# w2's row pairs one by one, its first piece in two halves of the partitions, c and x in three transfers each

## The chip, the cores, the metric

One core of one Trainium2 chip. Times are device microseconds (us) of whole executions. The profile is one execution taken by the hardware profiler; its span runs from the first to the last instruction and is about 2 us shorter than the time.

## The reference

A decoding step for one token: a condition `c` gives six modulation vectors; a layer norm, attention over a cache of 32,768 positions (32 query heads, 8 key and value heads of 128), a projection; then a second layer norm and a feed-forward layer of 1792 units. Only the sizes matter here: 149.4 MB are read once, and there is little arithmetic for each byte.

```python
mod = (silu(c) @ w_mod).reshape(1, 6, 1, -1)     # sa, ca, ga, sb, cb, gb
h = layernorm(x) * (1 + ca) + sa
x = x + ga * attention(h, k_cache, v_cache, wq, wo)
h = layernorm(x) * (1 + cb) + sb
x = x + gb * (maximum(h @ w1, 0) @ w2)           # w1 (512, 1792), w2 (1792, 512)
```

## The kernel before

Every load goes through one queue, in one fixed order, issued by SyncE: w_mod, c, x, wq, the K and V cache, wo, w1, w2. wo, w1 and w2 come in pieces of falling size, so that the arithmetic behind the last byte is short.

```python
FB = 2; FA = FT // FB                                    # 14 row blocks of w2 = 7 row pairs
W2P = [(0, 2, slice(0, FB)), (2, FA - 5, slice(0, FB)), (FA - 3, 1, slice(0, FB)), (FA - 2, 1, slice(0, FB)),
       (FA - 1, 1, slice(0, 1)), (FA - 1, 1, slice(1, FB))]
W1P = [(0, KT - 1), (KT - 1, KT)]
# ... in load():
    a0, n, bs = W2P[key[1]]
    # t: [128, n, nb, 512] in the slot of w1 and w2
    src = w2_v[:, a0:a0 + n, bs]
stream_dma(t[:], src)                                    # all kinds of loads
# ...
stream_dma(cx_row[0:8], c[0].rearrange("(a n) -> a n", a=8))
stream_dma(cx_row[8:16], A_x[0, 0].rearrange("(a n) -> a n", a=8))
```

The end of the program: w1's product, ReLU into `hid_bd`, then w2's product in 56 matmuls, which wait for w2 piece by piece. `keep_clock(n)` issues n matmuls whose result nobody reads; what it is meant for is in its name (in the run keep_clock, five more went with a clock of 1.00 in place of 0.50 behind them).

```python
for part, (k0, k1) in enumerate(W1P):
    w1_f = need(("w1", part))...
    for kt in range(k0, k1):
        for ft in range(FT):
            nc.tensor.matmul(hidT_ps[:, ft:ft + 1], lhsT=w1_f[...], rhs=h2T[:, kt:kt + 1], ...)
        if kt < KT - 2:
            keep_clock(1)
nc.scalar.activation(out=hid_bd ..., in_=hidT_ps ..., func=ACT.Relu)
keep_clock(1)
for part, (base, n, bs) in enumerate(W2P):
    w2_sb = need(("w2", part))
    # 8 matmuls for a row pair: out ffn_ps [4, 128]
# o_rows = ffn_ps * gb_rows; o_bf = o_rows + x1_rows
nc.sync.dma_start(out=out[0, 0]..., in_=o_bf[:])
```

Of the kernel before, what the change touches and what calls it, by code (L numbers as in the profile page):

```python
# [17 lines left out]
def kernel(  # L18
# [15 lines left out]
    P = 128  # L34
# [16 lines left out]
    FB = 2  # L51
    FA = FT // FB

    W2P = [(0, 2, slice(0, FB)), (2, FA - 5, slice(0, FB)), (FA - 3, 1, slice(0, FB)), (FA - 2, 1, slice(0, FB)),
           (FA - 1, 1, slice(0, 1)), (FA - 1, 1, slice(1, FB))]
    W1P = [(0, KT - 1), (KT - 1, KT)]
    assert Dh == 128 and REP == 4 and D == 512 and Dff % (FB * P) == 0 and NTILE == 4
    scale = float(Dh) ** -0.5
# [9 lines left out]
    def wo_v(i):  # L68
        g0, n = WOP[i]
        return A_wo[g0 * REP * Dh:(g0 + n) * REP * Dh, :].rearrange("(p r) d -> p r d", p=P)  # L70
# [24 lines left out]
    def piece(name, at, n):  # L95

        if name not in pieces:
            pieces[name] = ring.tile([P, 2 * TK * Dh], BF16, tag="slot", name=name)
        return pieces[name][:, at:at + n]

    def load(key):
        kind = key[0]
        if kind == "wm":
            t = ring.tile([P, KT, 6 * D], BF16, tag="slot", name="wm_sb")
            src = wm_v
        elif kind == "wq":
            t = ring.tile([P, KT, Hq * Dh], BF16, tag="slot", name="wq_sb")
            src = wq_v
        elif kind in "kv":
            g, steps = key[1], key[2]  # L110
            src = (kv if kind == "k" else vv)[g, :, TK * steps[0]:TK * (steps[-1] + 1), :]
            name = "Ksb" if kind == "k" else "Vsb"
            if len(steps) == 2:
                t = ring.tile([P, TK * len(steps), Dh], BF16, tag="slot", name=name)
            else:
                t = piece(name, TK * Dh * (steps[0] % 2), TK * Dh).rearrange("p (j d) -> p j d", d=Dh)
        elif kind == "wo":
            g0, n = WOP[key[1]]
            t = piece("wo_sb", g0 * REP * D, n * REP * D).rearrange("p (r d) -> p r d", d=D)
            src = wo_v(key[1])  # L120
        elif kind == "w1":
            k0, k1 = W1P[key[1]]
            t = piece("w12_sb", k0 * Dff, (k1 - k0) * Dff).rearrange("p (kt f) -> p kt f", f=Dff)
            src = w1_v[:, k0:k1]
        else:
            a0, n, bs = W2P[key[1]]
            nb = bs.stop - bs.start
            t = piece("w12_sb", KT * Dff + (a0 * FB + bs.start) * D, n * nb * D)
            t = t.rearrange("p (a b d) -> p a b d", a=n, b=nb)
            src = w2_v[:, a0:a0 + n, bs]  # L130
        stream_dma(t[:], src)
        if kind in "kv":
            for i, u in enumerate(steps):
                loaded[(kind, g, u)] = t[:, TK * i:TK * (i + 1), :]
        else:
            loaded[key] = t[:]

    def stream_dma(dst, src):
        i = nc.sync.dma_start(out=dst, in_=src)  # L139
        tc.stamp_issue_order_token(i.ins, "sp_stream")  # L140
        if last_loop:

            tc.add_manual_dep(i.ins, last_loop[0], mybir.DependencyInfo(
                mybir.DependencyClass.NoSync, mybir.DependencyReason.DATA))
# [5 lines left out]
    stream += [("v", LAST, (0, 1)), ("v", LAST, (2,)), ("v", LAST, (3,))] + [("wo", i) for i in range(len(WOP))]  # L150
    stream += [("w1", i) for i in range(len(W1P))] + [("w2", i) for i in range(len(W2P))]
    pos = [0]

    def need(key):
        while key not in loaded:
            load(stream[pos[0]])
            pos[0] += 1
        return loaded[key]
# [1 line left out]

    wm_sb = need(("wm",))
    cx_row = const.tile([16, D // 8], BF16)
    stream_dma(cx_row[0:8], c[0].rearrange("(a n) -> a n", a=8))
    stream_dma(cx_row[8:16], A_x[0, 0].rearrange("(a n) -> a n", a=8))

    ident_bf = const.tile([P, P], BF16)
    make_identity(nc, ident_bf[:])
# [8 lines left out]
    for hp in range(4):  # L176
        h, par = hp // 2, hp % 2
        src = AP(ib.tensor, ib.offset + 64 * h + par, [[ib.ap[0][0], P], [0, 4], [2, 32]])
# [67 lines left out]
    def bank(name):  # L246
        return ps_s.tile([P, 512], F32, tag="s", name=name)[:]
# [360 lines left out]
    with tc.manual_schedule(engines={mybir.EngineType.PE, mybir.EngineType.DVE}):  # L608
# [125 lines left out]
        ffn_ps = bank("ffn_ps")[0:KT, 0:P]  # L734
        last = len(W2P) - 1
        for part, (base, n, bs) in enumerate(W2P):
            w2_sb = need(("w2", part))
# [43 lines left out]
```

## Time and profile before

| | |
|---|---|
| time, median of 6 runs (lowest to highest) | 355.96 us (355.69 to 356.53) |
| span | 353.7 us |
| share of the DMA engines' time that packets took | 98.4% |

(The prediction was made from the first three runs, with a median of 355.84.) The DMA engines are busy to the end; the prediction shows the lines. This table, by stretches of the tail: start and end of the stretch, its length, busy us (and instructions) of each engine, granted TensorE clock, busy share of the DMA engines, GB/s.

```profile
core 0: us, PE busy (x) PEld busy (x) DVE busy (x) ACT busy (x) POOL busy (x), PEclk, DMA share, GB/s
344.00:346.00 2.00, 2.00 (x42) 1.23 (x41) 0.57 (x3) 0.12 (x1) 0.00 (x0) 1.00 1.03 400
346.00:348.00 2.00, 1.53 (x42) 1.49 (x40) 0.00 (x0) 0.29 (x1) 0.00 (x0) 1.00 1.04 396
348.00:350.00 2.00, 1.84 (x34) 1.71 (x32) 0.00 (x0) 0.00 (x0) 0.00 (x0) 1.00 0.57 209
350.00:352.00 2.00, 0.71 (x13) 0.53 (x10) 0.56 (x2) 0.00 (x0) 0.00 (x0) 1.00 0.00 0
```

The DMA moves 400 and 396 GB/s up to 348 us and has moved its last byte before 350.

### The profile page before, as it was taken

The numbers are of one execution on the slowest core, as the hardware profiler recorded it, in microseconds if no ns is written. First come the engines' busy times: TensorE is split into PE (matmuls) and PEld (weight loads), VectorE is DVE, ScalarE is ACT, GpSimd is POOL, SyncE is SP. The second block draws the span as 40 slices with busy tenths as digits, with TensorE's granted clock in tenths as the row PEclk, the third lists the DMA queues.
The fourth block names the chain that finished last, engine by engine and source line by source line (L and its number), as shares of the span: only waits on it lengthen the run. The fifth ranks groups of instructions, "written<-read, shape, count | busy, mean of one in ns | idle before, by whom it ended". The sixth has DMA issues, their size and how long they took to land. (4 is left out here: it accounts for less than half of the span.)

```text
span 353.7 us, 4064 instructions
## 1 busy us (share of the span) xinstructions
PE 278.1 (79%) x1348; PEld 111.8 (32%) x1351; DVE 207.3 (59%) x269; ACT 28.2 (8%) x68; POOL 8.5 (2%) x14
## 2 busy tenths in 40 slices
PE   0352781999898979897969797979789787989995
PEld 0121230333343423332323233333333233334445
DVE  8555774882868268472949177553938095743050
ACT  1212004000110011001100101010100010020000
POOL 9000000000000000000000000000000000000000
PEclk9995997799899999999999998999999999999999
DMA  8999999999999999999999999999999999999994
GB/s 317 450 419 452 432 412 437 448 419 424 459 419 422 445 437 421 437 441 419 437 448 419 424 459 416 426 436 437 422 434 445 426 424 448 430 422 422 423 418 186
DMA packets 7076, 149.59 MB, mean 423 GB/s; under 512 B 792, under 2 KB 1048, under 8 KB 2200
## 3 DMA queue, kind: packets, MB, share of 16 engines
q1 hardware_dynamic: 7064, 149.43, 98.4%
q8 instruction: 8, 0.13, 0.1%
q14 instruction: 4, 0.03, 0.0%
HBM read 149.42 MB, written 0.00 MB: 422 GB/s over the span
## 5 line engine op out<-in xcount | busy, mean ns | idle before, releaser
L411 DVE STREAM_TRANSPOSE KTt<-Ksb 128x2048 f32<-128x2048 f32 x64 | 143.2, 2283 | 66.5 <-DMA Ksb<-in_A_k_cache_dram 58.8
L493 PE MATMUL o_ps<-Vsb,PT_g 128*16 (+1 forms) x512 | 128.0, 382 | 22.4 <-ACT qbd L395 9.5
L431 PE MATMUL S_ps<-KTt,qbd 128*128 128x512 bf16 x512 | 122.5, 391 | 22.2 <-DVE KTt L411 20.6
L431 PEld LDWEIGHTS <-qbd 128*128 128x128 bf16 x512 | 49.0, 98 | 87.0 <-issue 29.1
L493 PEld LDWEIGHTS o_ps<-Vsb,PT_g 128*16 x416 | 35.9, 86 | 90.7 <-issue 66.4
L437 DVE TENSOR_SCALAR_CACHE_REDUCE S_g<-S_ps 128x512 f32<-128x512 f32 x16 | 11.0, 690 | 27.7 <-PE S_ps L431 27.7
L395 ACT COPY qbd<-qrep_sb 32x128 bf16<-32x128 bf16 x32 | 9.4, 295 | 139.0 <-PE S_ps L431 137.9
L474 DVE STREAM_TRANSPOSE PT_g<-P_g 128x1024 bf16<-128x1024 bf16 x8 | 9.7, 1218 | 6.6 <-ACT P_g L468 6.6
L465 ACT ACTIVATE nbias<-Mb_ps 128x1 f32<-128x1 f32 x8 | 1.4, 171 | 131.1 <-PE Mb_ps L463 131.1
L493 PEld LDWEIGHTS <-PT_g 128*16 128x16 bf16 x96 | 8.2, 90 | 11.0
L233 PE MATMUL xc_ps<-cx_sel,cx_bd 16*128 16x2 bf16 x4 | 0.3, 172 | 12.8 <-DVE cx_bd L227 12.8
L468 ACT ACTIVATE P_g<-S_g,nbias 128x1024 bf16<-128x1024 f32 x8 | 9.2, 1148 | 0.2
L524 DVE SCALAR_TENSOR_TENSOR Y<-o_ps,smask,Y 16x128 f32<-16x128 f32 x24 | 8.1, 339 | 0.8
L179 DVE COPY sel<-ident_bf 128x128 bf16<-128x128 bf16 x4 | 7.6, 3730 | 0.0
L480 PE MATMUL L_ps<-Lexp,ones_f 128*128 128x4 f32 x16 | 3.0, 257 | 4.3 <-DVE Lexp L477 4.3
L606 PE MATMUL spare_ps<-qbd,ident_bf 128*128 128x512 bf16 x16 | 5.1, 380 | 0.2 <-issue 0.2
L449 PE MATMUL mT_ps<-ident_f,m_p 128*1 128x128 f32 x8 | 2.2, 270 | 3.9 <-DVE m_p L446 2.0
L452 DVE TENSOR_REDUCE Mrow<-mT_ps 1x4 f32<-1x128 f32 x8 | 2.1, 257 | 5.3 <-PE mT_ps L449 5.3
L480 PEld LDWEIGHTS L_ps<-Lexp,ones_f 128*128 128x128 f32 x16 | 3.1, 222 | 5.7 <-issue 5.1
L543 DVE TENSOR_TENSOR oT_sb<-acc_ps,Linv 128x4 bf16<-128x4 f32 x8 | 1.2, 151 | 5.7 <-PE acc_ps L530 5.7
L514 DVE MEMSET o_ps<- 16x512 f32 x8 | 3.9, 485 | 0.8
L561 DVE CAST o_sb<-o_ps 128x4 bf16<-128x4 f32 (+2 forms) x4 | 0.7, 166 | 6.1 <-PE o_ps L557 6.1
(112 smaller groups left out, 85.2 us busy)
## 6 DMA issues: line engine op xcount, KB each, us to landing
Ksb<-in_A_k_cache_dram SPq DMA_DIRECT2D x16, 4096.0 KB, 29.2
Vsb<-in_A_v_cache_dram SPq DMA_DIRECT2D x15, 4096.0 KB, 24.5
wq_sb<-in_A_wq_dram SPq DMA_DIRECT2D x1, 4096.0 KB, 18.8
Vsb<-in_A_v_cache_dram SPq DMA_DIRECT2D x2, 2048.0 KB, 23.4
wm_sb<-in_w_mod_dram SPq DMA_DIRECT2D x1, 3072.0 KB, 10.4
wo_sb<-in_A_wo_dram SPq DMA_DIRECT2D x1, 2048.0 KB, 25.1
w_sb<-in_B_w_dram SPq DMA_DIRECT2D x1, 1344.0 KB
wo_sb<-in_A_wo_dram SPq DMA_DIRECT2D x1, 1024.0 KB, 27.0
```

The costliest lines, as they stand in the source:

```text
L179: nc.vector.tensor_copy(out=sel[:, hp, :].rearrange("p (a c) -> p a c", a=4), in_=src)
L395: nc.scalar.copy(out=o, in_=i)
L411: t = nc.vector.transpose(out=KTt[:].bitcast(F32), in_=Ksb[:, 32 * half:32 * half + 32, :].rearrange("p j d -> p (j d)").bitcast(F32),)
L431: nc.tensor.matmul(S_ps_tiles[g], lhsT=qbd[g % 2][:, hp, s, :], rhs=KTv[:, 16 * sl:16 * sl + 16, h, :, par], start=(t4 == 0 and sl == 0 an ...
L437: nc.vector.tensor_scalar(out=S_tiles[g][:, G, :], in0=S_ps_tiles[g], scalar1=1.0, scalar2=None, op0=ALU.mult, op1=ALU.max, accum_out=m_ti ...
L468: nc.scalar.activation(out=P_g[:], in_=S_g[:].rearrange("p g f -> p (g f)"), func=ACT.Exp, bias=nbias[:], scale=scale, accum_out=l_g[:],)
L474: nc.vector.transpose(out=PT_g[:], in_=P_g[:])
L480: nc.tensor.matmul(L_ps[:], lhsT=ones_f[:], rhs=Lexp[:], start=True, stop=True)
L493: nc.tensor.matmul(o_tiles[g][:], lhsT=PT, rhs=Vx, start=False, stop=False, skip_group_check=True)
L514: nc.vector.memset(o_tiles[g][:], 0.0)
L524: nc.vector.scalar_tensor_tensor(out=Y[:], in0=o[:, s], scalar=smask[:, s:s + 1], in1=Y[:], op0=ALU.mult, op1=ALU.add,)
L606: nc.tensor.matmul(spare[0], lhsT=ident_bf[:], rhs=qbd[0][:, 0, 0:4, :], start=True, stop=True)
```

## The change

The intent: TensorE waited for a 512 KB piece of w2 (row pairs 2 and 3), so these come one by one. And the transfers take eight semaphores in turn, which the end of the program waits for in a fixed order; six more transfers put the output on the last of them. One of the six comes from the row pairs, four from c and x, and one from cutting w2's first piece into partitions 0 to 63 and 64 to 127.

```diff
-    W2P = [(0, 2, slice(0, FB)), (2, FA - 5, slice(0, FB)), (FA - 3, 1, slice(0, FB)), (FA - 2, 1, slice(0, FB)),
-           (FA - 1, 1, slice(0, 1)), (FA - 1, 1, slice(1, FB))]
+    W2P = [(0, FA - 5, slice(0, FB))] + [(a, 1, slice(0, FB)) for a in range(FA - 5, FA - 1)]
+    W2P += [(FA - 1, 1, slice(b, b + 1)) for b in range(FB)]
@@
-        stream_dma(t[:], src)
+        if key == ("w2", 0):
+            for half in (slice(0, P // 2), slice(P // 2, P)):
+                stream_dma(t[half], src[half])
+        else:
+            stream_dma(t[:], src)
@@
-    stream_dma(cx_row[0:8], c[0].rearrange("(a n) -> a n", a=8))
-    stream_dma(cx_row[8:16], A_x[0, 0].rearrange("(a n) -> a n", a=8))
+    for at, row in ((0, c[0]), (8, A_x[0, 0])):
+        rows = row.rearrange("(a n) -> a n", a=8)
+        for a0, a1 in ((0, 3), (3, 6), (6, 8)):
+            stream_dma(cx_row[at + a0:at + a1], rows[a0:a1])
```

## The prediction

What no trace or run had shown is rival (a), that the two halves of the partitions run at half rate, and the terms that rested on it. The sum without those terms is the one that stands: −0.26 us, 355.6. With them, an engine's 8 runs of a half (0.64 us) take twice their time in one half or in both, +0.64 to +1.28 us, less the 0.09 and 0.22; that came to about +0.3 to +1.0 us, so 356.2 to 356.8. The prediction weighed it at somewhat under one half and set 355.7 between the two. The 0.06 us for c and x is an estimate, four more small packets of 16 ns each on an engine. In the trace of before, a run of 2048 bytes took 84 ns and one of 32,768 bytes 1213, where the prediction has 80 and 1209.

> **What bounds the kernel now.** I read the page's slices first, then the chain that ended last, then the tail instruction by instruction, and last the queue of the engine that issues the transfers.
>
> ```profile
> span 353.7 us, 4064 instructions
> DMA  8999999999999999999999999999999999999994
> q1 hardware_dynamic: 7064, 149.43, 98.4%
> DMA 12%; PE 1%; DVE 0%; SPq 0%; issue 0%
> ```
>
> The 16 DMA engines are busy in every slice but the last, 98.4% of the span, and 149.43 MB pass through them. Nothing that the change does in the first 340 us can shorten this; it can only leave a hole in it or fill it. What is left is the last slice. The chain in order of time:
>
> ```profile
> 305.94 25.65 DMA Vsb<-in_A_v_cache_dram
> 331.59 0.02 issue
> 331.61 16.67 DMA w_sb<-in_B_w_dram
> 348.28 0.04 issue
> 348.32 2.41 PE ffn_ps L742 x40
> 350.73 0.02 issue
> 350.75 0.29 DVE o_rows L747
> 351.04 0.02 issue
> 351.06 0.28 DVE o_bf L749
> ```
>
> The w2 transfer issued at 331.61 (512 KB, row pairs 2 and 3, the second piece of w2) lands at 348.28; forty matmuls, two vector instructions and the output follow without a hole. So the end hangs on the landing of w2's second piece, not on its last. The timeline says how long TensorE stood:
>
> ```profile
> 347.11 1.05 PE L742 MATMUL ffn_ps<-w_sb,hid_bd 128*4 128x128 bf16 x16 [0.47 <-ACT hid_bd L728]
> 348.32 2.39 PE L742 MATMUL ffn_ps<-w_sb,hid_bd 128*4 128x128 bf16 x40 [0.15 <-DMA w_sb<-in_B_w_dram]
> 351.37 0.29 SPq L750 DMA_DIRECT2D out_dram<-o_bf  x1
> ```
>
> The 0.15 us counts from a modelled end. The single starts lie 55.5 ns apart, the sixteenth is at 347.944, so the seventeenth could have started at 348.00: 0.32 us were lost. The landings (last of the 16 updates of each piece's semaphore) are 346.98, 348.28, 348.92, 349.52, 349.85 and 350.20. TensorE reaches the pieces after the second at 349.21, 349.66, 350.10 and 350.33, each later than its landing: from 348.32 it works without a stop. The last piece allows 350.24, only 0.09 us before TensorE comes to it.
>
> After the output is issued, 2.35 us remain to the end of the span:
>
> ```profile
> L776 SPq EVENT_SEMAPHORE  x8: 17/28/783, 351.7 to 353.7; - x8
> L776 SPq DRAIN  x3: 7/7/7, 352.8 to 353.1; - x3
> SPq L776 <- DMA out_dram<-o_bf: 0.8, 1, 0.8
> ```
>
> The 50 transfers take eight semaphores in turn; the output is the 50th and so has the second. SyncE's closing waits come in a fixed order, up to two semaphores each. The second wait instruction holds the output's semaphore, starts at 351.77 and ends at 352.55 (the 783 ns above). Four more waits, long satisfied, start at 352.59, 352.66, 352.72 and 352.78, and the drain at 352.85. Those 0.29 us stand behind the output for nothing.
>
> [...] Every w2 piece before spans 128 partitions, so no number of this trace agrees or disagrees; this is the largest open question. [...] the 8-row transfers of c and x left nine updates each, one early one and eight from data[...].
>
> **The change part by part.**
>
> *c and x in six transfers instead of two.* Four more issues of about 0.4 us (0.37 and 0.28 us, starts 0.4 apart), so wq goes out near 3.5 us instead of 1.9. w_mod keeps the engines busy until about 9.7 us: hidden. The first K load becomes the ninth transfer and shares w_mod's semaphore, so it can't be issued before w_mod lands (11.14 us, was issued at 2.33). wq's 4 MB fill the engines until about 20 us and issue to first packet took 1.0 us at the start: hidden too. On an engine, one such small packet with its completion took some 16 ns (two of them between 9.684 and 9.715 us)[...]. c and x landed at 10.87 us but VectorE touches them at 12.07, so a few tenths are free. Sum on the path: 0 to +0.06 us.
>
> *w2's row pairs 2 and 3 apart.* Same bytes, same order, 2048-byte runs as before (80 ns each). Row pair 2 should land half-way between 346.98 and 348.28, at about 347.63. TensorE then goes through: row pair 2 from 348.00, 3 from 348.44, 4 not before its landing (348.96), 5 from 349.56, the halves of 6 from 350.00 and 350.24, where the last landing holds it. The last group started at 350.33; the gain is 0.09 us, not 0.32, because TensorE has caught up with the DMA.
>
> *w2's first piece in two halves of 64 partitions.* One more completion (about 10 ns an engine) and one more wait on TensorE (51 ns, beside the wait for hid_bd that ends there too). If halves run at full pace: 0 to +0.05 us. [...]
>
> *The waits for a free semaphore.* A transfer waits for the eighth before it. With eight w2 pieces, the last two wait for w1's two parts, which landed at 344.60 and 345.66. Issued then, with about 1.0 us to the first packet, they are there at 345.7 and 346.7; the earliest engine wants the last one at about 347.9. No hole, 1.2 us to spare.
>
> *The output's semaphore.* Six more transfers make it the 56th, eighth in turn, which the closing waits name in the fifth wait instruction of two, just ahead of the drain. From its end to the drain there would be about 0.07 us instead of 0.29: −0.22 us.
>
> [...] −0.09 − 0.22 + 0.05 = about −0.26 us. Time before 355.84, so 355.6. [...]
>
> **Rivals.** (a) [...] the data runs here go at a constant 27.1 GB/s an engine (32,768 bytes in 1.209 us)[...]. Against: engines are up to 2 us apart in the tail (the last piece's updates run from 348.24 to 350.20), and early ones lose only slack; and the pieces were evidently chosen by someone who tuned this tail. It would give 356.2 to 356.8. (b) *The order of the closing waits is not fixed by semaphore* but by what the program used last; then the output may again sit in the middle and the 0.22 us vanish: about 355.8. (c) *TensorE's whole 0.32 us comes back*, if the small pieces land earlier than I interpolate: 355.3. The landings bound it, and the queue moved 396 GB/s between 346 and 348 us, so I give it little. (d) *The last two pieces come too late* since they now wait for w1: a hole of some tenths in the DMA's last 3 us. The 1.2 us to spare speak against it.
>
> **Range and chances.** All outcomes lie within 1.3 us, 0.4% of the time, and the three runs before spread over 0.84 us. [...] set 355.7, between the two but nearer the first; 355.1 to 356.7 holds both with the scatter of the runs. Two per cent would be 7.1 us, twice the whole stretch from hid_bd to the output: faster by that is not possible, slower only by an accident such as an idle queue that I don't see.
>
> **What would show it.** Right: the chain's last DMA piece is w2's last half, landing within 0.1 us of 350.20, and TensorE's 56 matmuls have holes of some hundredths each at single pieces; SyncE's long closing wait is followed by the drain within 0.1 us. Rival (a): the two half pieces land together near 347.6 to 348.3 instead of 346.98, everything after them shifts with them, and the rate between 344 and 348 us falls below the 396 to 400 GB/s of before. Rival (b): several short waits still follow the long one. Rival (d): idle DMA share near 348 us. My prediction is wrong if the time moves by over 1 us in either direction; then a transfer in the long stream has lost its place in the queue.

## The result and the profile after

358.81 us, median of 6 runs (358.45 to 359.72), against 355.96 of the kernel before. The ratio is 1.0083, 95% interval 1.0067 to 1.01: slower, by 2.9 us, and outside the range predicted. Ratios here and below are the mean time of one kernel's runs over that of the other's runs of the same rounds, so they are not quite the ratio of the medians quoted.

The chain that ended last, in order of time, from the issue of w2's second half on:

```profile
331.76 17.36 DMA w_sb<-in_B_w_dram
...
349.20 4.93 PE ffn_ps L749 x56
...
354.15 0.29 DVE o_rows L754
```

Before, the corresponding wait ended at 348.28 and forty matmuls were left, 2.41 us. Now all 56 stand behind one wait, which ends at 349.11, and they take 4.93 us. The table by stretches:

```profile
344.00:346.00 2.00, 1.68 (x32) 0.89 (x31) 0.64 (x4) 0.26 (x1) 0.00 (x0) 1.00 1.09 293
346.00:348.00 2.00, 1.25 (x37) 0.98 (x34) 0.00 (x0) 0.03 (x1) 0.00 (x0) 1.00 1.00 255
348.00:350.00 2.00, 0.80 (x8) 0.83 (x9) 0.00 (x0) 0.27 (x1) 0.00 (x0) 0.81 1.01 351
350.00:352.00 2.00, 2.00 (x21) 2.00 (x20) 0.00 (x0) 0.00 (x0) 0.00 (x0) 0.50 0.32 114
```

Two things are new. The DMA engines are fully busy (1.09, 1.00) but move 293 and 255 GB/s instead of 400 and 396: each packet takes longer. The trace's record of single packets says the same: runs of 2048 bytes took 84 ns each before, and 121 to 155 ns (medians of half microseconds) from 344.5 to 347 now. Runs of w1, 3584 bytes over all 128 partitions, went from 140 to between 225 and 240 ns in that stretch, so transfers beside the halves took longer as well. And the granted clock is 0.50 from 349.25 to 352.66, a stretch of 3.41 us. The timeline of TensorE:

```profile
347.37 0.50 PE L728 MATMUL hidT_ps<-h2T,w_sb 128*128 128x1 bf16 x14 [0.62 <-DMA w_sb<-in_B_w_dram]
349.20 4.91 PE L749 MATMUL ffn_ps<-w_sb,hid_bd 128*4 128x128 bf16 x56 [1.33 <-DMA w_sb<-in_B_w_dram]
```

It waits for w1's last part, then 1.33 us for w2's first piece, and then works at half clock: starts of the 128-column matmuls lie 106 ns apart up to 352.67 and 55 ns after that. The closing waits are the part that went as intended:

```profile
L783 SPq EVENT_SEMAPHORE  x8: 17/28/28, 355.1 to 356.7; - x8
SPq L783 <- DMA out_dram<-o_bf: 0.5, 1, 0.5
```

SyncE still waits for the output, only later in its list. Before, the second instruction held the output's semaphore and was recorded with 783 ns; now the output's (108) is in the sixth, and the trace shows the wait as a gap ahead of it: the fifth ends at 355.398, the sixth starts at 355.957, and the drain follows at 356.025.

Where the 3.1 us of the span come from, by three marks of the two traces (TensorE's first w2 matmul, the first instruction on the finished product, the end):

| stretch | before | after | difference |
|---|---|---|---|
| start of the span to the first w2 matmul | 347.11 | 349.20 | +2.09 |
| first w2 matmul to the product's end (PE's last piece of the chain) | 347.11 to 350.73: 3.62 | 349.20 to 354.13: 4.93 | +1.31 |
| from there to the end of the span | 350.73 to 353.72: 2.99 | 354.13 to 356.79: 2.66 | −0.33 |

### The profile page after: what moved, and what is told of

It is laid out like the page before. It is cut to its first block, busy times and chain, and to the rows that moved or that the text cites. A ratio compares the mean times of both kernels' runs of the same rounds, so it can differ in the third digit from the quotient of the medians.

```text
span 356.8 us, 4072 instructions
## 1 busy us (share of the span) xinstructions
PE 282.6 (79%) x1348; PEld 115.0 (32%) x1351; DVE 207.5 (58%) x269; ACT 28.2 (8%) x68; POOL 8.5 (2%) x14
## 2 busy tenths in 40 slices
DMA packets 7109, 149.61 MB, mean 419 GB/s; under 512 B 824, under 2 KB 1080, under 8 KB 2232
## 5 line engine op out<-in xcount | busy, mean ns | idle before, releaser
L500 PE MATMUL o_ps<-Vsb,PT_g 128*16 (+1 forms) x512 | 129.7, 391 | 22.2 <-ACT qbd L402 9.7
L438 PE MATMUL S_ps<-KTt,qbd 128*128 128x512 bf16 x512 | 124.5, 396 | 19.5 <-DVE KTt L418 17.9
L500 PEld LDWEIGHTS o_ps<-Vsb,PT_g 128*16 x416 | 36.9, 89 | 91.2 <-issue 66.0
L749 PE MATMUL ffn_ps<-w_sb,hid_bd 128*4 128x128 bf16 x56 | 4.9, 273 | 1.3 <-DMA w_sb<-in_B_w_dram 1.3
L749 PEld LDWEIGHTS <-hid_bd 128*4 128x4 bf16 x56 | 4.8, 110 | 1.4 <-ACT hid_bd L735 1.4
```

The costliest lines, as they stand in the source:

```text
L438: nc.tensor.matmul(S_ps_tiles[g], lhsT=qbd[g % 2][:, hp, s, :], rhs=KTv[:, 16 * sl:16 * sl + 16, h, :, par], start=(t4 == 0 and sl == 0 an ...
L500: nc.tensor.matmul(o_tiles[g][:], lhsT=PT, rhs=Vx, start=False, stop=False, skip_group_check=True)
L749: nc.tensor.matmul(ffn_ps, lhsT=hid_bd[:, ft, i, :], rhs=w2_sb[:, a, b - bs.start, i * P:(i + 1) * P], start=(part == 0 and a == 0 and b = ...
```

## The experiments

The theory after the comparison: (1) a transfer to partitions 0 to 63, or 64 to 127, runs slower than one over all 128, down to half the rate, and slows those next to it (in the trace, 121 to 155 ns instead of 84 for 2048 bytes, 225 to 240 instead of 140 for w1's runs); (2) the clock of 0.50 (called the half clock from here on) goes back to the late landing, which made TensorE wait for 1.33 us, and costs once more. Both were guesses to be tested; why the halves should be slower, no run shows. The numbers ahead of the word "Rival" are the theory's. Rivals: the number or size of the transfers; the six small ones of c and x; the changed waits for a free semaphore; for (2), a half clock that comes at this point by chance.

The kernel before ran again beside each group of experiments, with a median of 11 runs each time: 355.97 us beside one_piece, row_split, halves_alone and keep_clock; 355.81 beside one_piece_55, cx_alone, wq_low and wq_mid; 355.74 beside the two extra and the first two act_delay runs; 355.75 beside act_delay_bare. Times come from four to six executions of an experiment, but a trace was kept of only one of them.

**one_piece.** The first piece whole again, and c in four transfers to keep the count of 56.

```diff
-        if key == ("w2", 0): ... two halves
+        stream_dma(t[:], src)
-        for a0, a1 in ((0, 3), (3, 6), (6, 8)):
+        for a0, a1 in ((0, 2), (2, 4), (4, 6), (6, 8)) if at == 0 else ((0, 3), (3, 6), (6, 8)):
```

> The changed kernel with w2's first piece again one transfer over 128 partitions; c goes in four transfers instead of three, so that there are still 56 transfers and the output is still the eighth in turn. Theory [...]: first piece lands near 347.1 us, no half-clock stretch at the end, time 355.4 to 355.7, 3 us under the changed kernel. Rival (the six extra transfers or the later waits for a semaphore delay the stream, whatever the partitions): still 358 or more.

Measured: 358.26 us, ratio 1.0074 (1.0057 to 1.009). The rival's number, but for a reason of the experiment's own. The queue of SyncE at the start, and the DMA a little later:

```profile
1.18 1.22 SPq L139 DMA_DIRECT2D cx_row<-in_c_dram  x4
...
11.07 0.36 SPq L139 DMA_DIRECT2D wq_sb<-in_A_wq_dram  x1
```

```profile
10.00:11.00 1.00, 0.00 (x0) 0.00 (x0) 1.00 (x7) 0.00 (x0) 0.00 (x0) 1.00 0.01 0
11.00:12.00 1.00, 0.00 (x0) 0.00 (x0) 1.00 (x8) 0.00 (x0) 0.00 (x0) 1.00 0.00 0
```

Seven small transfers make wq the ninth. It takes w_mod's semaphore and can't be issued before w_mod has landed, at 11.05 us. The DMA stands for over 2 us, and every later load is late by that much: w1's first part was issued at 324.99 against 321.91 before, and the time is 2.3 us longer. Nothing in the tail is slow: the DMA moves 395 to 402 GB/s there and the clock is 1.00. The run says nothing about the partitions, but it shows that six small transfers are exactly what this start bears.

**one_piece_55.** The same without the seventh.

```diff
-        if key == ("w2", 0): ... two halves
+        stream_dma(t[:], src)
```

> The changed kernel with w2's first piece again one transfer over 128 partitions and nothing put in its place: 55 transfers, wq the eighth as in the changed kernel, the output the seventh in turn. In one_piece wq had become the ninth and had to wait for w_mod's landing (issued at 11.07 instead of 3.2 us), which is a fault of that experiment. Theory [...]: 355.4 to 355.8, the tail as before. Rival (the six small transfers or the single row pairs cost something of themselves): 356.5 or more.

Measured: 355.62 us, ratio 1.0007 (0.999 to 1.0024), no different from before. The last landing is 350.26. Undoing the cut by partitions, and with it one transfer, takes away the whole loss.

**row_split.** Still two transfers of 256 KB in place of the first piece, but cut by row pair.

```diff
-    W2P = [(0, FA - 5, slice(0, FB))] + [(a, 1, slice(0, FB)) for a in range(FA - 5, FA - 1)]
+    W2P = [(a, 1, slice(0, FB)) for a in range(FA - 1)]
-        if key == ("w2", 0): ... two halves
+        stream_dma(t[:], src)
```

> The changed kernel with its first w2 piece cut in two by row pair (two transfers of 256 KB over all 128 partitions) instead of by partitions; still 56 transfers, each of the same bytes. Theory (it is the partitions): as one_piece, 355.3 to 355.7. Rival (it is the number or the size of the transfers, or that TensorE waits for two of them): as the changed kernel, 358 to 359.

Measured: 355.52 us, ratio 0.9991 (0.9978 to 1.0004). With 56 transfers, the same bytes in each and the output on the last semaphore, the loss is gone, so it isn't in number or size. Timeline and stretches:

```profile
347.06 3.60 PE L745 MATMUL ffn_ps<-w_sb,hid_bd 128*4 128x128 bf16 x56 [0.45 <-ACT hid_bd L731]
```

```profile
344.00:346.00 2.00, 2.00 (x42) 1.25 (x42) 0.57 (x3) 0.11 (x1) 0.00 (x0) 1.00 1.03 397
346.00:348.00 2.00, 1.55 (x42) 1.49 (x41) 0.00 (x0) 0.29 (x1) 0.00 (x0) 1.00 1.05 399
```

Its span is 353.3 us, 0.4 shorter than before; in time the interval reaches just past 1. It is the best version found, but not clear of the scatter.

**halves_alone.** The kernel before, only its first w2 piece cut by partitions.

```diff
-        stream_dma(t[:], src)
+        if key == ("w2", 0): ... two halves, as in the change
+        else: ... as before
```

> The kernel before with only its first w2 piece cut into partitions 0 to 63 and 64 to 127. Theory: the whole loss and more, because the closing waits save less: 358.3 to 359.3, 2048-byte runs of 110 to 155 ns between 344 and 348 us, first piece landing near 349. Rival (c and x in six transfers, or row pairs one by one, bear part of the loss): under 357.5.

Measured: 359.51 us, ratio 1.0091 (1.0075 to 1.0108), 3.5 us longer than before. The two halves landed at 348.27 and 349.21.

```profile
344.00:346.00 2.00, 1.57 (x33) 0.91 (x32) 0.57 (x3) 0.14 (x1) 0.00 (x0) 1.00 1.07 274
346.00:348.00 2.00, 1.23 (x36) 0.96 (x33) 0.00 (x0) 0.28 (x1) 0.00 (x0) 1.00 1.02 239
348.00:350.00 2.00, 0.66 (x7) 0.69 (x8) 0.00 (x0) 0.01 (x1) 0.00 (x0) 0.54 1.03 341
```

Here the half clock began at 348.14 and lasted two stretches, to 354.97, so the 56 matmuls took 5.95 us. The halves alone bear the loss. (The expected time was 358.3 to 359.3. The traced execution, at 360.05 one of the two slowest, had the second stretch of half clock; of the others no trace was kept.)

**keep_clock.** The changed kernel with work for TensorE in its wait.

```diff
         keep_clock(1)
+        keep_clock(5)
```

> The changed kernel with five more filler matmuls (about 1.1 us) on TensorE between hid_bd and the w2 product, in the 1.2 us in which it waits for the halves. Theory [...]: granted clock 1.0 from 349 to the end, the 56 matmuls 55 ns apart, time 357.0 to 357.5. Rival (the half clock comes at this point whatever TensorE does): no change, 358.5 to 359.

Measured: 357.25 us, ratio 1.0033 (1.0017 to 1.0048), 1.56 under the changed kernel's 358.81 by the medians (of different rounds). The DMA is as slow as in the changed kernel (271 and 240 GB/s between 344 and 348 us); the clock isn't:

```profile
347.87 1.24 PE L613 MATMUL spare_ps<-qbd,ident_bf 128*128 128x512 bf16 x5
349.06 3.35 PE L750 MATMUL ffn_ps<-w_sb,hid_bd 128*4 128x128 bf16 x56
```

```profile
348.00:350.00 2.00, 2.00 (x22) 1.25 (x21) 0.00 (x0) 0.19 (x1) 0.00 (x0) 1.00 1.03 344
350.00:352.00 2.00, 2.00 (x38) 1.97 (x36) 0.00 (x0) 0.00 (x0) 0.00 (x0) 1.00 0.45 161
```

Five matmuls whose result nobody reads took the 56 useful ones from 4.91 to 3.35 us. So the loss has two parts, the late landing and the clock, of about half each.

**cx_alone.** The kernel before with c and x in three transfers each.

```diff
-    ... two transfers of 8 rows
+    ... for each of c and x, three transfers of 3, 3 and 2 rows, as in the change
```

> The kernel before with only c and x in three transfers each: 54 transfers, the output the sixth in turn. Theory: no cost within the scatter, 355.7 to 356.1, first K load issued at about 11 us without a hole in the DMA's work. Rival (the late first K load [...] delay the stream): 356.5 or more.

Measured: 356.06 us, ratio 1.0008 (0.9991 to 1.0026). No cost to be seen. The first K load went out at 11.21 us, the sixteenth landing of wq was at 20.84 and of that K load at 30.51, against 20.77 and 30.45 before. (In the profiled run the clock was at 0.5 from 295.59 to 302.42 us, and TensorE came 1.3 us late to the w2 product. All fifteen traces have such stretches at one place or another before 305 us, that of before from 26.22 to 36.46 for one; what brings those was not tested.)

**wq_low and wq_mid.** wq's 4 MB in three transfers of 1, 2 and 1 MB (in other order), which differ in where they are cut. The author expected about half the rate in all three of wq_low, but in wq_mid in the outer two alone; that the middle one, partitions 32 to 95, would run at full rate was an assumption, which no trace had shown so far.

```diff
+        if kind == "wq":
+            for p0, p1 in ((0, 64), (64, 96), (96, 128)):      # wq_low
+            for p0, p1 in ((0, 32), (32, 96), (96, 128)):      # wq_mid
+                stream_dma(t[p0:p1], src[p0:p1])
```

> The kernel before with wq's 4 MB in three transfers, partitions 0-63, 64-95 and 96-127[...]. [...] all 4 MB at about half the rate, 215 to 230 GB/s while they run, landing near 30 us instead of 20.8, time about 9 to 10 us longer. Rival (a transfer over fewer than 128 partitions is slow per se, or three transfers are): wq_mid is as slow as this one.

> As wq_low, again 1, 2 and 1 MB, but cut at partitions 0-31, 32-95 and 96-127[...]. [...] only the outer two run at half rate, the middle one at 420 to 435 GB/s, time 4.5 to 5.5 us longer than before, about half of wq_low's loss. Rival: as slow as wq_low.

Measured: 366.64 us for wq_low (ratio 1.0308, 1.0293 to 1.0323) and 363.18 for wq_mid (1.0208, 1.0187 to 1.0228), 10.8 and 7.4 us longer than before. wq was complete at 31.64 and 28.71 us. wq_low is about as expected, somewhat over the 9 to 10; wq_mid lies between the theory (5) and the rival (10.8). The stretches of wq_mid suggest why:

```profile
18.00:20.00 2.00, 1.51 (x11) 0.44 (x6) 0.62 (x1) 0.59 (x1) 0.00 (x0) 1.00 0.99 426
20.00:22.00 2.00, 1.26 (x10) 0.97 (x10) 1.29 (x10) 0.00 (x0) 0.00 (x0) 1.00 1.53 344
22.00:24.00 2.00, 0.17 (x2) 0.00 (x0) 0.92 (x2) 0.26 (x1) 0.00 (x0) 1.00 0.87 180
```

While all engines are in the middle transfer it moves 426 GB/s, twice the 180 to 262 that wq_low shows; but engines are up to 3 us apart here (the middle's landings run from 21.20 to 24.14), and I take it, without proof, that the ones ahead in the next, outer transfer disturb the others. The packets do slow down: the 41 of 32,768 bytes that started between 17 and 20 us took 1213 to 1219 ns, the 21 between 20 and 22 us 2584 in the median. A single transfer between full ones is the cleaner test.

**extra_low and extra_mid.** The kernel before with one more load of 512 KB between x and wq, into partitions 0 to 63 or 32 to 95 of an unused tile. Bytes, runs (8192 bytes) and number of partitions are the same; the rows read from the K cache shift with the partitions.

```diff
+    extra = const.tile([P, 4096], BF16, name="extra")
+    stream_dma(extra[lo:lo + 64], A_k_cache[0, 0]...[lo:lo + 64, 0:4096])      # lo = 0 or 32
```

> The kernel before with one more load of 512 KB of the K cache into partitions 0 to 63 of an unused tile (8 KB rows), between c and x and wq. [...] 512 KB at half rate, and neighbours' engines disturbed as well: 2.4 to 3.5 us longer, about 1.2 to 2.3 us more than extra_mid. Rival (cost of a 64-partition transfer whatever its partitions): the same as extra_mid.

> The same 512 KB into partitions 32 to 95[...]. [...] no more than its bytes, 512 KB at 430 GB/s = 1.2 us longer (0.9 to 1.7). Rival: as extra_low.

Measured: 359.08 us for extra_low (ratio 1.0086, 1.0072 to 1.01) and 356.9 for extra_mid (1.0037, 1.002 to 1.0053): 3.3 and 1.2 us longer. First extra_low, then extra_mid:

```profile
10.00:11.00 1.00, 0.00 (x0) 0.00 (x0) 1.00 (x7) 0.00 (x0) 0.00 (x0) 1.00 1.06 189
11.00:12.00 1.00, 0.00 (x0) 0.00 (x0) 1.00 (x8) 0.00 (x0) 0.00 (x0) 1.00 0.98 205
```

```profile
10.00:11.00 1.00, 0.00 (x0) 0.00 (x0) 1.00 (x7) 0.00 (x0) 0.00 (x0) 1.00 1.02 427
11.00:12.00 1.00, 0.00 (x0) 0.00 (x0) 1.00 (x8) 0.00 (x0) 0.00 (x0) 1.00 1.22 524
```

(A packet's bytes count where it starts, so single microseconds scatter.) All 64 packets of 8192 bytes took 309 ns each in extra_mid. In extra_low so did the first ten, which started before 10 us; the 54 after them took 624 in the median (359 to 931). And w_mod, the full transfer ahead, landed at 12.54 us in extra_low, at 11.17 in extra_mid, at 11.14 before. So 64 partitions are not slow in themselves (309 ns into 32 to 95), and even into partitions 0 to 63 the first ten packets ran at full pace (309 ns), the others at half of it in the median (624); what parts the two is not shown. The full transfer beside them, w_mod, was 1.4 us late too, which fits that 512 KB cost 3.3 us and not the 2.4 of a halved rate (an estimate: 512 KB at half of the 430 GB/s seen in the stream).

**act_delay and act_delay_fill.** For the clock: row_split, with its full transfers, and TensorE made to wait by a longer ScalarE stage; the second with filler in the wait.

```diff
+        late = rows_sb("late")...                      # [128, 14, 73], read by nobody
+        nc.scalar.copy(out=late, in_=hidT_ps[:].unsqueeze(2).to_broadcast([P, FT, 73]))
         nc.scalar.activation(out=hid_bd ..., func=ACT.Relu)
         keep_clock(1)
+        keep_clock(5)                                  # act_delay_fill only
```

> row_split (355.5 us, all transfers over 128 partitions) with one more ScalarE copy of 128x1022 before hid_bd, so that TensorE stands for about 1.1 us longer before the w2 product while the DMA is left as it is. Theory [...]: the 56 matmuls start near 348.2, a stretch at half clock of 3.4 us follows, 357.4 to 358.2. Rival (the half clock came with the halves or by chance): 56 matmuls 55 ns apart, end set by 348.2 + 3.1, 356.1 to 356.5.

> act_delay with five filler matmuls on TensorE in that pause. Theory: clock stays 1.0 to the end, 356.1 to 356.5. Rival: no different from act_delay.

Measured: 357.18 us for act_delay (ratio 1.0031, 1.0014 to 1.0047; single runs 355.84 to 357.5) and 356.74 for act_delay_fill (1.0015, 1.0 to 1.003). The first lies between what theory and rival expected, the second above its 356.1 to 356.5, and the two intervals overlap: the times decide nothing. In the one trace of act_delay the theory's expectation fell:

```profile
348.73 3.29 PE L747 MATMUL ffn_ps<-w_sb,hid_bd 128*4 128x128 bf16 x56 [1.11 <-ACT hid_bd L733]
```

TensorE stood 1.11 us and the clock stayed at 1.00 in that trace, so a pause of a microsecond doesn't always bring the half clock. (The traced execution took 356.46 us; four of the other five took 357.18 to 357.5, and whether the clock fell in those is not on record.) In all traces the clock's whole periods last 3.41 us or a multiple of it (in that of before 3.41, 6.83, 10.24, 20.48 us and longer). I then counted, from the shapes in the traces, the columns that TensorE's matmuls streamed in each stretch of 3.41 us. In the stretch ahead of the half clock it was 676 in the changed kernel and 1080 in halves_alone; in the stretch of act_delay with the pause it was 3357, of keep_clock 3114, of before 2360, and no half clock followed these. w1's matmuls stream one column each; 512 columns come from every filler, and in act_delay 2304 from the 18 matmuls of w2 that fell into the same stretch.

The count is not a rule, though. Earlier in these very traces the half clock also followed stretches with more columns than the 2360 that kept it: 2568 in before (from 213.95 us) and 3080 in cx_alone (from 292.18). Nor do the recorded idle times part the cases: TensorE was idle for 33% of act_delay's stretch, which kept the clock, and for 29% of act_delay_bare's below, which did not.

**act_delay_bare.** act_delay without its last three fillers.

```diff
-                if kt < KT - 2:
-                    keep_clock(1)
...
-        keep_clock(1)
```

> act_delay without its last three filler matmuls (two in the w1 product, one behind it), still no transfer over half the partitions. Counted over the clock's 3.41 us stretches, the changed kernel streamed 676 columns and halves_alone 1080 in the stretch ahead of the half clock; before 2360, keep_clock 3114 and act_delay 3357, and no half clock followed. Theory [...]: under about 1500 columns in a stretch near 346 to 349, then 0.5, matmuls 106 ns apart for up to 3.4 us, median 357.8 to 359.5. Rival (the half clock needs the halves): no stretch at 0.5 behind 340 us, 356.9 to 357.4 as act_delay.

Measured: 357.08 us, ratio 1.0045 (1.0029 to 1.0061). No transfer is slow, and the half clock is there, from 347.26 to 350.67, after a stretch with 1208 columns:

```profile
344.71 1.48 PEld L724 LDWEIGHTS <-w_sb 128*128 128x128 bf16 x56 [0.48 <-DMA w_sb<-in_B_w_dram]
347.63 4.72 PE L744 MATMUL ffn_ps<-w_sb,hid_bd 128*4 128x128 bf16 x56 [1.35 <-ACT hid_bd L731]
```

The 56 matmuls took 4.72 us instead of act_delay's 3.29. So the halves aren't needed for it. What brings it isn't shown: the columns were fewer ahead of it here (1208) than in keep_clock, which kept the clock (3114), but that is no rule, as said above, and the times of act_delay and act_delay_bare (357.18 and 357.08) don't differ. The time came out under the expected 357.8 to 359.5: TensorE reached the product at 347.63, 1.1 us earlier than in act_delay's trace, which I had not counted. 0.7 us of that is that act_delay's trace was already late at w1's first matmul (345.41 against 344.71, after a half clock from 295.10 to 298.51); the missing fillers account for at most the rest.

## Why the prediction was wrong

- **The bound** was read rightly for the kernel before: the landing of w2 sets the end. It did not stay so. In the changed kernel the last piece landed at 351.99 and the product ended at 354.13: from the first piece's landing on TensorE, and no longer a landing, set the end.
- **The choice between the rivals** was the first fault. The prediction named slow halves as rival (a) and then weighed them at somewhat under one half, because engines are up to 2 us apart and "the pieces were evidently chosen by someone who tuned this tail". The second is no evidence about the hardware, and the first seems to have made the loss larger (next point). What the prediction gave for the rival had been shown by no trace; the packet times of extra_low and extra_mid show the halved rate afterwards (8192 bytes: 624 ns in the median into partitions 0 to 63 from 10 us on, 309 into 32 to 95). The sign that the prediction had set for it came too: 293 and 255 GB/s between 344 and 348 us.
- **The size of rival (a)** failed at the step by which the last landing slips by 0.64 to 1.28 us. The last landing went from 350.20 to 351.99, by 1.79, and the first piece from 346.98 to 349.11, by 2.13 (its halves landed at 348.24 and 349.11, not together near 347.6 to 348.3). The step counted only the halves' own packets at double time. In the trace, w1's runs beside the halves are slower too (225 to 240 ns instead of 140), and its last part landed at 347.32 instead of 345.66: the last engine in w1 was 1.66 us later before it came to its halves.
- **TensorE's speed** was the missing term: rival (a)'s sum took 55 ns a matmul for granted. From the first to the last start, 55 steps at 55.5 ns would have been 3.05 us; they took 4.70, so the half clock cost 1.65. Before, the same took 3.38, because of the 0.33 us hole that the single row pairs were to close; the difference is the +1.31 of the table. keep_clock, 1.56 us faster with only fillers added, agrees.
- **w2's row pairs one by one**: right. In row_split row pair 2 landed at 347.62 (347.63 interpolated) and the last piece at 350.21; the product's end moved only from 350.73 to 350.68 in the trace, as the landing of row pair 5 (349.57), with 16 matmuls behind it, holds it.
- **c and x in six transfers**: right. wq went out at 3.23 us, the first K load at 11.04 after w_mod's landing, without a hole; cx_alone is no slower. one_piece shows how close this was: one small transfer more and wq itself waits.
- **The waits for a free semaphore**: right as to the hole; the last two pieces waited for w1 (issued at 345.08 and 347.34 as w1 landed late) and the DMA stayed busy.
- **The output's semaphore**: right. From the end of the wait that holds it to the drain it was 0.29 us (352.55 to 352.85) and is 0.04 (355.985 to 356.025); measured from the issue of the output to the drain, 1.47 and 1.25, the predicted 0.22. Another 0.11 us of the table's −0.33 fell behind the drain: TensorE's own drain took 134 ns before and 13 now, and row_split has that too. Why is open.
- **Its sign of being wrong**, a move of over 1 us, came, but not for the reason given with it: no transfer lost its place in the queue (w1's first part was issued at 322.05, against 321.91 before).
- **Two sums** are off without consequence: the outcomes named lie 1.5 us apart (355.3 to 356.8), not 1.3, and 7.1 us is about one and a half times the stretch from hid_bd (346.73) to the output's issue (351.37), not twice.

What stays open: what exactly brings the half clock (neither columns nor recorded idle time part the stretches here), why transfers to partitions 0 to 63 and 64 to 127 are slow, and why engines are 1 to 2 us apart at the end of the stream (348.24 to 350.20 in the last piece of before).

## What to carry to other kernels

Cut a transfer along bytes within the partitions rather than into the lower and the upper half of them: here, at equal bytes and equal count, the cut by row pair was free (ratio 0.9991) and the kernel with the cut into partitions 0-63 and 64-127 was 3.3 us slower (358.81 against 355.52), part of it in the transfers next to it. When a change can make TensorE wait near the end, price the matmuls behind the wait at both clocks (55 and 106 ns apart here), and try work for TensorE in the wait (1.56 us here).
